# Pairs in the first layer's projections, one mask fewer on GpSimd, and the third layer's first weights listed earlier

## The chip, the cores and the metric

The kernel runs on one core of a Trainium2 chip. The metric is the time of one execution on the device, in microseconds; lower is better. Five engines matter: TensorE (PE, whose weight loads are listed as PEld), VectorE (DVE), ScalarE (ACT), GpSimd (POOL), and SyncE (SP), whose queue issues the DMAs.

## The reference

Three layers in float32, over 4 batches of 576 positions.

- First layer: attention with a feature map. For each of 8 heads, k and q (64 wide) are projected on 128 features, the largest absolute value of each row is subtracted, and exp of both signs is taken. From k come kv (features by values) and z (their sum); the output is q'kv / (q'z + 1e-6).
- Second layer: four attention experts of one head each (causal softmax); each position takes the two experts with the largest gate logits, weighted by a softmax over these two.
- Third layer: eight two-layer experts, 512 to 1024 to 512 with relu. A position's expert is its argmax, or the expert of the position before it where a local gate says so; the output is scaled by that expert's softmax value.

```
e = fresh_e if s == 0 or local_gate[b, s] < 0.5 else prev_e
out[b, s] = p[e] * (np.maximum(x[b, s] @ w1[e], 0.0) @ w2[e])
```

## The kernel before, in words

Instructions are written in program order and put into engine queues by a scheduler that goes by their order in the program as priority, and by when it thinks their inputs are ready. Each engine then works through its queue in order.

**First layer** (class PhaseA). The work is 16 units, one for two heads of one batch, and the steps of three units are interleaved by A_STEPS. `proj` (line 245) projects k ("k", four tiles), the last positions of both ("e", one tile) and q ("q", four tiles): for every tile t there is one matmul per head h, on the upper or the lower 64 rows of the array, into the PSUM tile pt[h]. The tiles of "k" and "q" rotate through five banks (tag X), those of "e" through two (tag mm). `num` (line 370) makes the numerators in two halves of 288 columns, in banks of tag mm, and copies each out to the batch's x1: the first by ACT (line 386), the second by DVE (line 384).

**Second layer** (PhaseB). Five slots run one after the other: s0, s1, x, s2, s3. A main slot works on the two experts that its batch uses most; slot x works on one further expert of one batch (the extra). Each slot is an order of steps written out by hand; that of s2 is

```
    "s2": ("s0b f s0a t t s1a s2a s1b f s2b p0a p0b t t s3a t s3b t p1a f t p1b t p2b p2a f f t p3a f p3b s4a n0 "
            "f v0 s4b p4a n1 t p4b S0a v1 S0b t o0 t S1a S1b o1 o2 o3 t t w"),
```

s is a score, p a transpose of its exponentials, f a projection of the next slot, v the product with the values, o two output products (`wout`, matmuls px in banks of tag mm), S a score of the next slot, and t a tick. `dest` moves px to the batch's x2. The extra's result y has to be added to the batch that it belongs to, which is known only at run time: for each batch b there is a factor hit[b], 1 for that batch and 0 for the others. Batch 0 is added on DVE in slot x itself (line 1274), batch 1 by `adds` on DVE (line 1291); for batches 2 and 3 `adds` writes y times hit to x2 on GpSimd, ahead of the slot (line 1284, sixteen instructions; that of batch 2 over y itself), and `dest` then adds px with a tensor_tensor on DVE (line 1230). `extras` sets hit of batch 3 to 0: it takes no extra.

**Background.** Gates, weight loads and splits run beside the slots. They are generators in lanes of a queue (class Background); a tick lets the first entry of each lane do one step, in the order of the lanes' letters. A `yield n` makes an entry wait n ticks (a plain one: the next tick), an entry with `after` waits until the named entry has left the queue, and `ensure` runs an entry to its end.

**The third layer's start.** `Gates.fresh` (line 593) counts how often each expert is wanted (cnt, line 624, on DVE), waits four ticks, sums the counts over the partitions with one small matmul (hpc, line 627), finds the most wanted expert with five DVE instructions (lines 630 to 635), casts its number (line 698) and has SP load it into a register. The first batch's gate g0 is put in lane r at the start of slot s2. With that register `weights_first` (entry W1_0) loads three pieces of the first weights, 512 KB each (line 1421), and splits each in a high part on ACT (line 1436, w1h) and a rest on DVE (line 1437, w1l). W1_0 is put in lane w at the start of slot s3, and the first f of that slot ensures it. `hidden` (line 1464) then multiplies: for each of 16 pieces 12 matmuls (ph, lines 64 to 66), of which ten pieces stand as f in slot s3. The layer's batches follow, each with 192 matmuls ph and 192 matmuls po on PE.

`Together` (line 69) puts the instructions of a block right behind the first one of them, with raised priority. `issue_after` orders the instructions of a block behind a given one on its engine.

Of the kernel before, what the change touches and what calls it, by code (L numbers as in the profile page):

```python
# [12 lines left out]
AF = mybir.ActivationFunctionType  # L13
OP = mybir.AluOpType
# [5 lines left out]
B, H, S, HD = 4, 8, 576, 64  # L20
# [5 lines left out]
HALF = S // 2  # L26
# [175 lines left out]
class PhaseA:  # L202
# [42 lines left out]
    def proj(self, i, nm):  # L245


        nc, r, after = self.nc, self.st[i], self.bg.tc.issue_after
        w, raws = self.w_phi, r["raw"]
        n = 1 if nm == "e" else 4  # L250
        u = r["u" + nm] = self.p3.tile([128, n, 256], F32, tag=f"u{nm}", name=f"u{nm}_{i}")
        mx = self.p3.tile([128, 2, n], F32, tag=f"mx{nm}", name=f"mx{nm}_{i}")
        if n == 1:
            pt = [self.ps.tile([128, HALF], F32, tag="mm", name=f"pj{nm}_{i}_{h}") for h in range(2)]
        else:
            pt = [self.ps.tile([128, 512], F32, tag="X", name=f"pj{nm}_{i}_{h}") for h in range(2)]
        for t in range(n):
            for h in range(2):
                p = slice(64 * h, 64 * h + 64)
                c = dict(k=0, e=512, q=640)[nm] + 128 * t  # L260
                with ExitStack() as x:
                    if i == 1 and nm != "k":
                        x.enter_context(after(self.kv_last.ins))
                    nc.tensor.matmul(pt[h][:, 128 * t:128 * t + 128], raws[p, c:c + 128], w[p], start=True, stop=True)  # L264
        for step in self.order(i, nm, n):
            if len(step) == 3:
                h, t0, t1 = step
                ins = lambda: nc.vector.tensor_reduce(
                    mx[:, h, t0:t1], pt[h][:, 128 * t0:128 * t1].rearrange("p (t f) -> p t f", f=NF),
                    axis=AX.X, op=OP.max, apply_absolute_value=True)  # L270
            else:
                h = step[0]
                ins = lambda: nc.vector.tensor_tensor(  # L273
                    u[:, :, NF * h:NF * h + NF], pt[h][:, 0:128 * n].rearrange("p (t f) -> p t f", f=NF),
                    mx[:, h, :, None].to_broadcast([128, n, NF]), op=OP.subtract)
            with ExitStack() as x:
                if i == 0 or i == 1 and nm == "k":
                    x.enter_context(after(self.last.ins))
                self.last = ins()
            if len(step) == 1:  # L280
                self.bg.anchor(self.last)
# [88 lines left out]
    def num(self, i, hf):  # L370
        nc, r, (b, p) = self.nc, self.st[i], self.units[i]
        qp, kvs = r["qp"], r["kvs"]
        if p == 0 and hf == 0:
            self.st["x1", b] = self.x1_tile(b)
            self.st["dd", b] = self.dr.tile([H, S], F32, tag="dd", name=f"dd_{b}", bufs=2)
        c = slice(hf * HALF, (hf + 1) * HALF)
        pn = self.ps.tile([128, HALF], F32, tag="mm", name=f"pn_{i}_{hf}")
        with Together(self.bg.tc) as one:
            for sg in range(2):
                for h in range(2):  # L380
                    one(nc.tensor.matmul(pn[64 * h:64 * h + 64, :], kvs[:, sg, 64 * h:64 * h + 64], qp[:, h, sg, c],  # L381
                                         start=sg == 0, stop=sg == 1))
        if hf:
            nc.vector.tensor_copy(self.st["x1", b][:, p, c], pn)
        else:
            nc.scalar.activation(self.st["x1", b][:, p, c], pn, AF.Copy)  # L386

    def den(self, i, hf):
        nc, (b, p) = self.nc, self.units[i]
# [92 lines left out]
class Gates:  # L482
# [110 lines left out]
    def fresh(self, xf, wg32, b, out):  # L593

        nc, ps, k, t = self.nc, self.ps, self.k, self.t
# [26 lines left out]
                                code[:, :, None].to_broadcast([128, QT, NE]), op=OP.is_equal)  # L622
        cnt = t([NE], "cnt8", b)
        nc.vector.tensor_reduce(cnt, hot.rearrange("p t e -> p e t"), axis=AX.X, op=OP.add)
        yield 4
        pc = ps.tile([128, HALF], F32, tag="mm", name=f"hpc_{b}")
        nc.tensor.matmul(pc[:, 0:NE], k.ones, cnt, start=True, stop=True)
        most, e0 = t([1], "most", b), out["e0"]
        c = t([NE], "cnt8", b)
# [424 lines left out]
class PhaseB:  # L1054
# [157 lines left out]
    def main(self, b, q):  # L1212
        nc = self.nc
        s = Slot(self, f"s{b}")
        s.q = q

        def early():
            s.ws = self.g[b]["ws"][:, :, 0:2]
            self.load_w(s, [self.gt.reg(self.g[b]["perm"][0:1, r:r + 1], f"b{b}_{r}", 3) for r in range(2)])
            yield  # L1220
            yield from self.split(lambda ch: self.x1[b][:, ch, :], q, f"b{b}", s.xs)

        def dest(hf, ch, c, px):
            if b not in self.x2:
                self.x2[b] = self.x2["pool"].tile([128, 4, S], F32, tag="x", name=f"x2_{b}")
            if q > self.qx and not (hf or ch):
                self.bg.ensure("adds")
            x2 = self.x2[b][:, ch, c]
            if q > self.qx:
                nc.vector.tensor_tensor(x2, px, x2, op=OP.add)  # L1230
            else:
                nc.scalar.activation(x2, px, AF.Copy)

        s.early, s.dest = early, dest
        return s

    def extra(self, q, nm, regs=None, entry=None):

        nc = self.nc
        s = One(self, nm)  # L1240
# [21 lines left out]
        def tile(b):  # L1262
            self.x2[b] = self.x2["pool"].tile([128, 4, S], F32, tag="x", name=f"x2_{b}")
            return self.x2[b]
# [12 lines left out]
            nc.vector.tensor_tensor(s.x2[:, ch, c], px, s.x2[:, ch, c], op=OP.add)  # L1277

        def adds():

            def scaled(x2, b):
                for ch in range(4):
                    for c in (slice(0, HALF), slice(HALF, S)):
                        nc.gpsimd.tensor_scalar(x2[:, ch, c], s.y[:, ch, c], self.hit[:, b:b + 1], 1.0,
                                                op0=OP.mult, op1=OP.mult)
                    yield

            for b in self.order[1:q]:
                m = self.hit[:, b:b + 1]
                for ch in range(4):  # L1290
                    nc.vector.scalar_tensor_tensor(self.x2[b][:, ch], s.y[:, ch], m, self.x2[b][:, ch],
                                                   op0=OP.mult, op1=OP.add)
                    yield
            for b in self.order[q + 2:]:
                self.bg.ensure(f"early_s{b}")
                yield from scaled(tile(b), b)
            yield from scaled(s.y, self.order[q + 1])

        s.adds = adds if entry is None else None
        s.early, s.dest = early, dest if entry is None else dest_one  # L1300
# [5 lines left out]
    def run(self, slots, order, pc):  # L1306
# [18 lines left out]
        for q, s in enumerate(slots):  # L1325
# [3 lines left out]
            early(q + 2, 9 if q == self.qx else 0)  # L1329
            if q == self.qx + 1:  # L1330
                bg.add("g0", pc.gate(0), False, lane="r")
                bg.add("adds", slots[self.qx].adds(), lane="a")
            if last:
                bg.add("sc", pc.scale(0), lane="r")
                bg.add("h", pc.gate2(0), lane="r")
                bg.add("W1_0", pc.weights_first(), False, lane="w", after=["g0"])
                bg.add("x0", pc.split(self.x2[0], "c0"), False, lane="w")

            def ready():
# [462 lines left out]
```

## Time and profile before

| | us |
|---|---|
| three runs | 545.13, 545.26, 545.91 (median 545.26) |
| the profiled execution | 545.53 |
| its span, first to last instruction | 543.7 |
| PE busy | 518.8 (95% of the span) |
| DVE busy | 362.4 (67%) |
| ACT busy | 263.6 (48%) |
| GpSimd busy | 159.0 (29%) |

The profile is of one execution; its instructions have their lines in the kernel, and idle time of an engine is put down to what ended it. Matmuls are pipelined, so PE's busy time covers stretches in which its instructions overlap. A float32 matmul stands as two records where its weights are float32. The granted clock of TensorE is 1.00 in nearly the whole span; 1.00 is 2.4 GHz and 0.50 is 1.2 GHz. The span divides into the first layer (to about 170 us), the second (to about 335 us, with the third layer's first matmuls from 302 us on) and the third.

### The profile page before, as it was taken

To read this page: it belongs to the slowest core of one execution; us is meant where nothing else is said; L and a number is where in the kernel's file an instruction comes from. 1 tells how busy PE (TensorE), PEld (TensorE's weight loads), DVE (VectorE), ACT (ScalarE), POOL (GpSimd) and SP (SyncE) were. 2 spreads that over 40 slices of the span, in tenths; PEclk is the share of its full clock that TensorE was granted. 3 is DMA by queue.
4 is the path that set the end of the run, shared out by engine and by line. 5 is a ranking of instruction groups with operands and counts; after the bars stand their busy time and mean duration, and the time that the engine had idled before them with its cause. 6 is when DMAs were issued, how large, how long until landed. Compare 5 with 4: busy or idle time off the path is not lost.

```text
span 543.7 us, 11808 instructions
## 1 busy us (share of the span) xinstructions
PE 518.8 (95%) x4456; PEld 437.6 (80%) x4456; DVE 362.4 (67%) x972; ACT 263.6 (48%) x603; POOL 159.0 (29%) x270
## 2 busy tenths in 40 slices
PE   7999999999999998999798899999999999999995
PEld 6766766666676787887586788999999999998995
DVE  7876777977754797987996767742764366527541
ACT  3867566656665467775755553431451235114100
POOL 5665696397477141222546010000000000000000
PEclk9999999999999999999999899999999999999999
DMA  8432373454125026402000601182335133813011
GB/s 245 133 112 88 109 234 101 147 153 156 27 74 182 5 68 184 138 2 79 2 1 10 225 0 47 33 261 99 131 133 177 45 127 133 270 45 127 2 55 39
DMA packets 32709, 57.07 MB, mean 105 GB/s; under 512 B 7012, under 2 KB 17636, under 8 KB 31620
## 3 DMA queue, kind: packets, MB, share of 16 engines
q1 hardware_dynamic: 32644, 56.24, 32.1%
q8 instruction: 37, 0.61, 0.5%
q14 instruction: 28, 0.23, 0.1%
HBM read 41.86 MB, written 14.36 MB: 103 GB/s over the span
## 4 chain that ended last, share of the span: by engine, by line
PE 70%; DVE 12%; ACT 9%; DMA 3%; issue 3%; POOL 2%; SPq 0%; ACTq 0%; DVEq 0%; POOLq 0%
PE po_c L64 6%; PE po_c L65 6%; PE po_c L66 6%; PE ph_c L64 5%; PE pq_s L766 5%; PE ph_c L65 5%; PE ph_c L66 5%; PE Y L332 3%; PE pd L398 3%; PE pn L381 3%; PE pjk L264 2%; PE py_s L913 2%; PE pt_s L885 2%; ACT a_kp L303 2%; DVE uk L273 2%
## 5 line engine op out<-in xcount | busy, mean ns | idle before, releaser
L64 PE MATMUL ph_c<-xh_c,w1h_c 128*128 128x288 f32 x256 | 77.4, 303 | 2.5 <-ACT w1h_c L1436 2.5
L65 PE MATMUL ph_c<-xl_c,w1h_c 128*128 128x288 f32 x256 | 76.2, 298 | 0.0
L64 PE MATMUL po_c<-h_c,w2h_c 128*128 128x288 f32 x256 | 76.1, 297 | 0.0
L66 PE MATMUL ph_c<-xh_c,w1l_c 128*128 128x288 f32 x256 | 75.9, 298 | 0.0
L65 PE MATMUL po_c<-h_c,w2h_c 128*128 128x288 f32 x256 | 75.5, 295 | 0.0
L1484 ACT ACTIVATE h_c<-ph_c 128x288 fp32r<-128x288 f32 x64 | 25.9, 408 | 102.2 <-PE ph_c L66 102.1
L66 PE MATMUL po_c<-h_c,w2l_c 128*128 128x288 f32 x256 | 75.4, 295 | 0.0
L308 POOL TENSOR_TENSOR zs<-a_kp 128x256 f32<-128x256 f32 x64 | 47.6, 757 | 52.9 <-ACT x L386 27.2
L64 PEld LDWEIGHTS ph_c<-xh_c,w1h_c 128*128 128x128 f32 x256 | 48.6, 190 | 4.6 <-ACT w1h_c L1436 2.7
L1485 DVE SCALAR_TENSOR_TENSOR h_c<-ph_c,h_c 128x288 fp32r<-128x288 f32 x64 | 29.0, 456 | 34.0 <-ACT h_c L1484 33.7
L64 PEld LDWEIGHTS po_c<-h_c,w2h_c 128*128 128x128 f32 x256 | 48.1, 188 | 0.9 <-issue 0.9
L65 PEld LDWEIGHTS ph_c<-xl_c,w1h_c 128*128 128x128 f32 x256 | 48.6, 190 | 0.0
L66 PEld LDWEIGHTS ph_c<-xh_c,w1l_c 128*128 128x128 f32 x256 | 48.4, 190 | 0.0
L66 PEld LDWEIGHTS po_c<-h_c,w2l_c 128*128 128x128 f32 x256 | 48.1, 188 | 0.0
L65 PEld LDWEIGHTS po_c<-h_c,w2h_c 128*128 128x128 f32 x256 | 48.1, 188 | 0.0
L766 PE MATMUL pq_s<-xh_b,w_s 128*128 128x288 f32 x192 | 43.6, 305 | 0.8 <-DVE q_s L733 0.4
L1507 DVE TENSOR_TENSOR fo_c<-po_c,pb 128x288 f32<-128x288 f32 x32 | 14.5, 455 | 42.6 <-PE po_c L66 42.6
L332 PE MATMUL Y<-a_kp,a_v 128*64 128x256 f32 x320 | 38.5, 384 | 0.5
L381 PE MATMUL pn<-qp,kvs 128*64 128x288 f32 x256 | 34.6, 408 | 0.3 <-ACT qp L368 0.3
L766 PEld LDWEIGHTS pq_s<-xh_b,w_s 128*128 128x128 f32 x192 | 32.0, 188 | 3.5 <-issue 1.3
L303 ACT ACTIVATE a_kp<-uk 128x1024 f32<-128x1024 f32 x30 | 31.6, 1052 | 6.4 <-DVE uk L273 3.4
L320 ACT ACTIVATE qp<-tr 128x512 f32<-128x512 f32 x64 | 33.6, 634 | 0.6 <-PE tr L318 0.6
(315 smaller groups left out, 1212.9 us busy)
## 6 DMA issues: line engine op xcount, KB each, us to landing
w1raw_c<-in_w_dram SPq DMA_DIRECT2D x16, 512.0 KB, 4.9
w2raw_c<-in_w_dram SPq DMA_DIRECT2D x16, 512.0 KB, 5.1
raw<-in_kq_dram SPq DMA_DIRECT2D x15, 320.0 KB, 3.2
rb<-d SPq DMA_DIRECT2D x32, 144.0 KB, 3.1
x1d<-x SPq DMA_DIRECT2D x4, 1152.0 KB
x2d<-x SPq DMA_DIRECT2D x4, 1152.0 KB
raw<-in_kq_dram SPq DMA_DIRECT2D x16, 256.0 KB, 4.4
a_v<-in_v_dram SPq DMA_DIRECT2D x16, 256.0 KB, 4.1
```

Of the source, the lines that this page charges most:

```text
L64: nc.tensor.matmul(out, lh, rh, start=start, stop=False, **kw)
L65: nc.tensor.matmul(out, lh, rl, start=False, stop=False, **kw)
L66: return nc.tensor.matmul(out, ll, rh, start=False, stop=stop, **kw)
L303: nc.scalar.activation(kp[:, 0:4, sg, :], u[:, 0:4, :], AF.Exp, scale=sc)
L308: add(zs[:, j, sg, :], kp[:, j, sg, :], kp[:, 2 + j, sg, :], op=OP.add)
L320: self.bg.anchor(nc.scalar.activation(qp[:, h, sg, 0:512], tp, AF.Exp, scale=sc))
L332: self.kv_last = one(nc.tensor.matmul(Y[64 * h:64 * h + 64, 0:256], vt[:, t, h, :], kp[:, t, :, h * NF:(h + 1) * NF], start=t == 0, stop=t ...
L381: one(nc.tensor.matmul(pn[64 * h:64 * h + 64, :], kvs[:, sg, 64 * h:64 * h + 64], qp[:, h, sg, c], start=sg == 0, stop=sg == 1))
L398: nc.tensor.matmul(pd[32 * h:32 * h + 32, :], r["kvs"][:, 2, o:o + 32], r["qp"][:, h % 2, sg, c], start=sg == 0, stop=sg == 1)
L766: self.nc.tensor.matmul(out, self.wqkv[t][:, wj, ch, 0:m], x[:, ch, c], start=wj == ch == 0 and x is xh, stop=wj == 1 and ch == 3)
L1484: nc.scalar.activation(hh[:, c], ph, AF.Relu),
L1485: nc.vector.scalar_tensor_tensor(hl[:, c], ph, 0.0, rd(hh[:, c]), op0=OP.max, op1=OP.subtract))
```

## The change

In `proj` the two heads of a tile become a pair, head 1 first, and each pair is ordered behind the one before. In `num` the two engines change places. In `fresh` the wait ahead of the sum is two ticks for batch 0 and four for the others. In `dest` of a main slot, slot s2 (q == qx + 1) computes x2 = x2 * hit + px in one DVE instruction, where x2 is y itself; slot s3 only copies px, the first half on ACT and the second on DVE; `adds` keeps batch 1 alone, and the sixteen GpSimd instructions of line 1284 are gone. W1_0 is put in lane w at the start of slot s2, behind g0.

```diff
         for t in range(n):
-            for h in range(2):
-                p = slice(64 * h, 64 * h + 64)
-                c = dict(k=0, e=512, q=640)[nm] + 128 * t
-                with ExitStack() as x:
-                    if i == 1 and nm != "k":
-                        x.enter_context(after(self.kv_last.ins))
-                    nc.tensor.matmul(pt[h][:, 128 * t:128 * t + 128], raws[p, c:c + 128], w[p], start=True, stop=True)
+            c = dict(k=0, e=512, q=640)[nm] + 128 * t
+            with ExitStack() as x:
+                if i == 1 and nm != "k":
+                    x.enter_context(after(self.kv_last.ins))
+                if t:
+                    x.enter_context(after(mm.ins))
+                one = x.enter_context(Together(self.bg.tc))
+                for h in (1, 0):
+                    p = slice(64 * h, 64 * h + 64)
+                    mm = one(nc.tensor.matmul(pt[h][:, 128 * t:128 * t + 128], raws[p, c:c + 128], w[p], start=True, stop=True))
...
         if hf:
+            nc.scalar.activation(self.st["x1", b][:, p, c], pn, AF.Copy)
+        else:
             nc.vector.tensor_copy(self.st["x1", b][:, p, c], pn)
-        else:
-            nc.scalar.activation(self.st["x1", b][:, p, c], pn, AF.Copy)
...
-        yield 4
+        yield 4 if b else 2
         pc = ps.tile([128, HALF], F32, tag="mm", name=f"hpc_{b}")
...
-            if q > self.qx and not (hf or ch):
-                self.bg.ensure("adds")
             x2 = self.x2[b][:, ch, c]
-            if q > self.qx:
-                nc.vector.tensor_tensor(x2, px, x2, op=OP.add)
+            if q == self.qx + 1:
+                if not (hf or ch):
+                    self.bg.ensure("adds")
+                nc.vector.scalar_tensor_tensor(x2, x2, self.hit[:, b:b + 1], px, op0=OP.mult, op1=OP.add)
+            elif q > self.qx and hf:
+                nc.vector.tensor_copy(x2, px)
             else:
                 nc.scalar.activation(x2, px, AF.Copy)
...
         def adds():
-
-            def scaled(x2, b):
-                for ch in range(4):
-                    for c in (slice(0, HALF), slice(HALF, S)):
-                        nc.gpsimd.tensor_scalar(x2[:, ch, c], s.y[:, ch, c], self.hit[:, b:b + 1], 1.0,
-                                                op0=OP.mult, op1=OP.mult)
-                    yield
-
             for b in self.order[1:q]:
...
-            for b in self.order[q + 2:]:
-                self.bg.ensure(f"early_s{b}")
-                yield from scaled(tile(b), b)
-            yield from scaled(s.y, self.order[q + 1])
...
             if q == self.qx + 1:
                 bg.add("g0", pc.gate(0), False, lane="r")
+                bg.add("W1_0", pc.weights_first(), False, lane="w", after=["g0"])
                 bg.add("adds", slots[self.qx].adds(), lane="a")
             if last:
                 bg.add("sc", pc.scale(0), lane="r")
                 bg.add("h", pc.gate2(0), lane="r")
-                bg.add("W1_0", pc.weights_first(), False, lane="w", after=["g0"])
```

## Rows read from the trace of the kernel before

**Rows 1.** The page: busy time by engine, and PE in 40 slices

```profile
PE 518.8 (95%) x4456; PEld 437.6 (80%) x4456; DVE 362.4 (67%) x972; ACT 263.6 (48%) x603; POOL 159.0 (29%) x270
...
PE   7999999999999998999798899999999999999995
```

**Rows 2.** Busy us by stretch: length, PE, PEld, DVE, ACT, POOL, PEclk, DMA, GB/s

```profile
100.00:120.00 20.00, 19.21 (x210) 13.17 (x210) 17.04 (x38) 14.67 (x31) 12.25 (x15) 1.00 0.61 190
...
260.00:280.00 20.00, 17.04 (x120) 13.60 (x121) 19.29 (x44) 12.73 (x40) 11.49 (x22) 1.00 0.01 1
280.00:300.00 20.00, 17.34 (x131) 13.96 (x128) 14.47 (x49) 10.23 (x33) 9.80 (x18) 1.00 0.07 20
300.00:320.00 20.00, 17.69 (x120) 16.38 (x121) 14.66 (x36) 11.26 (x25) 1.12 (x4) 0.91 0.40 140
```

**Rows 3.** Waits of PE: total us, times, longest us

```profile
PE ph_c L64 <- ACT w1h_c L1436: 2.5, 1, 2.5
...
PE pc L561 <- DVE cnt L558: 1.3, 2, 1.0
PE px_s L64 <- DVE x L1230: 1.1, 2, 0.8
...
PE pg L500 <- DVE x L1274: 0.8, 1, 0.8
...
PE pje L264 <- DVE x L384: 0.6, 1, 0.6
```

**Rows 4.** The chain of waits, 292 to 303 us: start, us, what

```profile
292.85 0.32 PE hpc L627 x2
...
297.62 3.56 DMA w1raw_c<-in_w_dram
301.20 1.06 ACT w1h_c L1436
302.31 0.41 PE ph_c L64
```

**Rows 5.** DVE in order of time: start, us

```profile
281.73 0.21 DVE L624 TENSOR_REDUCE cnt<-hot 128x8 f32<-128x40 f32 x1
...
296.42 0.13 DVE L698 CAST ri_c<-c_e 1x1 int32<-1x1 f32 x1
...
302.29 1.23 DVE L1437 TENSOR_TENSOR w1l_c<-w1raw_c,w1h_c 128x1024 fp32r<-128x1024 f32 x1 [1.19 <-ACT w1h_c L1436]
```

**Rows 6.** ACT in order of time, at the end of slot s2

```profile
299.74 0.63 ACT L1189 ACTIVATE woh_s<-wor_s 128x512 fp32r<-128x512 f32 x1 [5.12 <-PE px_s L65]
```

**Rows 7.** Busy us by stretch around the fall of the clock

```profile
302.80:306.10 3.30, 3.30 (x15) 2.99 (x14) 2.15 (x3) 1.96 (x4) 0.00 (x0) 0.50 0.60 195
306.20:308.00 1.80, 1.80 (x16) 1.80 (x16) 1.41 (x3) 1.66 (x4) 0.00 (x0) 1.00 0.25 68
```

**Rows 8.** The adding of the extra to batch 0 on DVE: ns min/median/max

```profile
L1274 DVE SCALAR_TENSOR_TENSOR x<-x,x_m,x x4: 805/1054/1056, 265.8 to 268.7; 128x576 f32<-128x576 f32 x4
```

**Rows 9.** GpSimd's masks: ns min/median/max

```profile
L1284 POOL TENSOR_SCALAR x<-x,x_m x16: 504/505/1003, 261.7 to 279.6; 128x288 f32<-128x288 f32 x16
```

**Rows 10.** PE in order of time: a unit of the first layer's steady part

```profile
43.91 1.16 PE L264 MATMUL pjk<-a_w,raw 64*128 64x128 f32 x16
44.91 0.39 PE L264 MATMUL pje<-a_w,raw 64*128 64x128 f32 x4
```

**Rows 11.** PE in order of time: a unit beside the second layer's gates

```profile
107.37 0.37 PE L264 MATMUL pjq<-a_w,raw 64*128 64x128 f32 x1
...
108.83 0.37 PE L264 MATMUL pje<-a_w,raw 64*128 64x128 f32 x1 [0.63 <-DVE x L384]
...
109.91 0.44 PE L358 MATMUL kvt<-ident,ue 128*128 128x128 f32 x2
```

**Rows 12.** DVE by line, 18 to 160 us: numerators' copies

```profile
L384 DVE COPY x<-pn 128x288 f32<-128x288 f32 x14 | 6.3, 453 | 13.3 <-PE pn L381 13.3
```

**Rows 13.** ACT by line, 18 to 160 us: numerators' copies

```profile
L386 ACT ACTIVATE x<-pn 128x288 f32<-128x288 f32 x14 | 5.5, 395 | 0.8 <-PE pn L381 0.8
```

## The prediction

> **What bounds the kernel now.** I read the page first: PE is busy in 95% of the span, and among the forty slices those below nine tenths lie at the start, at the end, at 204 us, and in a dip between 258 and 313 us [rows 1]. The table by stretch says how deep it is: PE is idle 2.96 us in 260 to 280, 2.66 us in 280 to 300 and 2.31 us in 300 to 320, beside 0.79 us in 100 to 120 [rows 2]. Outside the dip a change that gives PE no less work can gain next to nothing; inside it there are 7.9 us. The waits of PE name what ended that idle time: one wait of 2.5 us for the first high part of the third layer's weights, and smaller ones for DVE [rows 3]. Then the chain of waits, in order of time: the small sum hpc at 292.85, DVE's search behind it, the weights' DMA from 297.62 for 3.56 us, ACT's split for 1.06 us, and the first ph at 302.31 [rows 4]. So that wait is the end of a chain that begins with hpc, and hpc stands late by order alone: its input cnt was ready at 281.73 + 0.21 = 281.94 us, 10.9 us earlier [rows 5].
>
> **The sum, and the load that hangs on it.** In slot s2 the gate's first seven steps take the first seven ticks; four ticks more put hpc at the eleventh, behind the last transposes, and two ticks put it at the ninth, behind the projections. The entry g0 leaves its lane a tick after the sum, and since lane r comes before lane w, W1_0 issues its first two loads at the tenth tick, the third load and the first split at the twelfth. On SP nothing else stands between, and the three buffers that the loads fill are those of slot s3's weights, read for the last time by projections that stand before the ninth tick. I estimate hpc at 283 to 285 us: not before cnt, 281.94, and about where those projections end. From hpc to the first ph the chain took 302.31 - 292.85 = 9.46 us [rows 4]; at that length the first weights are split by 292.5 to 294.5 us, five us or more before PE is through with px, whose matmuls end about 2.47 us before the first ph. The wait goes whole: **-2.5 us**. The bounds are 0 and that wait.
>
> The splits move too: three of 1.06 us on ACT [rows 4] and three of 1.23 us on DVE [rows 5]. They used to lie where PE had stopped; now they lie in 290 to 300 us, among the ends of slot s2. ACT has room, it was idle 5.12 us just there [rows 6], and DVE was busy 14.47 of 20 us in 280 to 300 [rows 2]. They can still stand in front of an eviction of px, and a split whose load has not landed holds back what is queued behind it. Against that, the search behind hpc leaves that place, and PE waited 1.1 us for the evictions there [rows 3]. I put the two against each other at **0**, between -1.1 and +1.23 (one DVE split in the way).
>
> Moved early, hpc may find cnt not ready, and PE's queue stands behind it. The second layer's gates have the same sum at two ticks: four of them, of which two waited, 1.3 us together and 1.0 us at the most [rows 3]. I take the mean, 1.3 / 4: **+0.3 us**, between 0 and 1.0.
>
> **The clock.** The granted clock was 0.50, the level of 1.2 GHz, in 302.80 to 306.10, right after PE had stood still for 2.47 us, and 1.00 again after it [rows 7]. In the slow stretch 15 matmuls began in 3.30 us, 0.220 each; after it 16 in 1.80 us, 0.1125 each. At full clock the fifteen take 1.7 us: **-1.6 us** if PE no longer stops, 0 if it stops elsewhere as long.
>
> **GpSimd's masks.** Sixteen instructions of 0.505 us (median) go [rows 9]. Their own time is beside the path; what counts is DVE next to them, since DVE is busy 19.29 of 20 us in 260 to 280 and PE waits for it there [rows 2, 3]. The adding of the extra to batch 0 took 1.055 us three times and 0.805 us the fourth time, when GpSimd had paused [rows 8]: 3 x 0.25 = 0.75 us, directly ahead of the gate's first matmuls, which waited 0.8 us for it [rows 3]. I take **-0.75 us**, between 0 and -1.5. The lower end is three whole masks, 3 x 0.505. The Trainium skill, SBUF — State Buffer, section Who interferes with whom, says that a DVE instruction with two SBUF inputs and a GpSimd instruction that reads SBUF cannot run together, and that the second waits until the first has finished. By that rule the term would be that lower end, and the sum 0.75 us lower; the trace shows half of it, and I go by the trace.
>
> DVE's new x2 * hit + px in slot s2 replaces an instruction of the same shape, and slot s3's eight sums become four copies on each engine: 0, hidden beside ph, as PE's idle time in that slot is gone from 320 us on (slices of 9 in rows 1).
>
> **The pairs.** In the steady part of the first layer the heads run as pairs already: sixteen records of pjk begin in 44.91 - 43.91 = 1.00 us [rows 10]. Only beside the gates the pairs break up. In the worst unit, e and q, twenty records, take from 107.37 to 109.91 = 2.54 us [rows 11], where 20 x 1.00 / 16 = 1.25 us would do: 1.3 us, of which 0.63 us is one wait for the numerators' copy on DVE. Four other places lose a pair's time or so, 2 x 1.00 / 16 = 0.125 us each. That bounds the gain at 1.8 us. But DVE is busy 17.04 of 20 us in that stretch [rows 2], so the chain there runs through DVE, and PE's saving is mostly waited away: I take a fifth, **-0.4 us**. The other end is a loss: a pair waits for the later of two banks, at the 0.63 us of that row once more, +0.6.
>
> **The numerators' copies.** The copies last 0.453 us on DVE and 0.395 on ACT [rows 12, 13]; each engine still does one of a unit's two, and PE works on beside them: 0. The second one, for whose bank e waited, now leaves by ACT; that is in the bound above.
>
> **The sum.** -2.5 + 0 + 0.3 - 1.6 - 0.75 - 0.4 = -4.95 us. The profiled execution took 545.53, of which 543.7 are its span; it stands 0.27 us above the median of 545.26. The forecast for the median is 545.26 - 4.95 = 540.3 us.
>
> **The rivals.**
>
> *The gap fills further.* With weights at hand from 293 us on, PE can put ph between the px that wait for evictions, and DVE's gain carries through. Then the terms go to their lower ends: 2.5 + 1.1 + 1.6 + 1.5 + 1.2 = 7.9 less, 537.4 us. For it: PE was idle 2.66 us in 280 to 300 [rows 2]. Against it: ph and px share two banks, and px has priority. 14%.
>
> *The gain is passed on.* PE no longer waits for weights, but for slot s2's last evictions behind DVE's splits; the wait is halved and the clock still falls, or DVE stays the bound in 260 to 300. I reckon half of the 4.95 us: 542.8 us. For it: DVE's 19.29 of 20 us. 20%.
>
> *The load is not earlier.* If SP reads the register or ACT takes the split no sooner (a split placed behind slot s2's exponentials in ACT's queue, the loads behind a buffer), the change doesn't do what it says, and only the terms of masks and pairs remain, -1.15: 544.1 us. Against it: nothing in SP's queue or in the buffers stands in the way. 10%.
>
> *Slower: the pairs stall.* Each pair is now issued as one, and PE's queue stands until both banks are free. If every unit then waits as the one of rows 11 did, 0.63 us in 15 units is 9.5 us, less the 4.95: 549.8 us. It decides from 4.95 / 15 = 0.33 us a unit. Against it: in the steady part no such wait stands among PE's [rows 3], and the banks change hands long before. For it: at the start DVE is the later one. 6%. The Trainium skill, TensorEngine Tiling (Array Packing), section Gotcha 1: PSUM Pressure, says that row tiles working side by side need banks of their own and that this raises the pressure on PSUM; that is this rival's mechanism, and the trace shows it in one unit of sixteen.
>
> **How the numbers follow.** The forecast's own case has 50%, from 539 to 541.8 us. The range, 537.4 to 544.2 us, takes in the first two rivals and the third one's centre; what lies outside is the slower rival and the tails, less than 2 in 10. A measurement of this kernel can tell some 0.2% (1.1 us) from no change. Faster by more: forecast and the first two rivals, 0.84. Within: the third, 0.10. Slower: 0.06.
>
> **What would show it.** Right: hpc near 284 us and the first w1raw issue near 288 us; no wait of ph for w1h over 0.5 us; a granted clock of 1.00 from 300 to 310 us; the adding of the extra at 0.8 us four times; pjq of one length in all units. Wrong: PE's idle time in 260 to 320 us still over 6 us, a stretch at 0.50 after the start, or waits of pj for copies in many units.

## The result, and the profile after the change

The changed kernel takes 540.25 us (median of 4 runs, 539.98 to 541.20) where the kernel before took 545.59 beside it (545.13 to 546.37): ratio 0.9904, 95% interval 0.9886 to 0.9921. The forecast was 540.3 us, range 537.4 to 544.2. The profiled execution took 539.98 us, of which 538.2 are its span.

The page of the changed kernel, its busy times, PE's slices and the granted clock, beside [rows 1]:

```profile
PE 516.0 (96%) x4456; PEld 436.2 (81%) x4456; DVE 359.3 (67%) x968; ACT 264.5 (49%) x607; POOL 150.2 (28%) x254
...
PE   7999999999999999999999899999999999999995
...
PEclk9999999999999999999999999999999999999998
```

The dip between 258 and 313 us has become one slice of 8. The stretches, with the columns of [rows 2]:

```profile
260.00:280.00 20.00, 17.78 (x125) 14.21 (x126) 19.12 (x51) 13.74 (x44) 1.98 (x7) 1.00 0.00 1
280.00:300.00 20.00, 18.30 (x141) 14.92 (x139) 16.54 (x42) 12.37 (x32) 10.00 (x17) 1.00 0.45 140
300.00:320.00 20.00, 19.56 (x153) 18.07 (x153) 14.65 (x46) 10.44 (x29) 1.41 (x5) 1.00 0.05 21
```

PE is idle 2.22 + 1.70 + 0.44 = 4.36 us here, where it was 7.93 before [rows 2]: 3.57 less. No stretch is at 0.50 any more (0.91 in 300 to 320 before). POOL's 11.49 us have become 1.98, since the masks are gone. The waits of PE over the whole run (total us, times, longest us):

```profile
PE pc L564 <- DVE cnt L561: 1.4, 2, 1.1
...
PE pje L267 <- DVE x L389: 1.1, 1, 1.1
...
PE px_s L64 <- DVE x L1233: 0.7, 1, 0.7
PE pd L401 <- DVE x L389: 0.7, 1, 0.7
...
PE pg L503 <- DVE q_s L736: 0.5, 1, 0.5
```

The wait of 2.5 us for the first weights [rows 3] is in no row, nor is a wait of hpc. Three instructions in order of time (start, us): DVE's count, PE's sum hpc, and the load in SP's queue:

```profile
279.88 0.22 DVE L627 TENSOR_REDUCE cnt<-hot 128x8 f32<-128x40 f32 x1
...
282.19 0.29 PE L630 MATMUL hpc<-cnt,ones 128*128 128x8 f32 x2
...
285.63 7.62 SPq L1414 DMA_DIRECT2D w1raw_c<-in_w_dram  x4
```

hpc runs at 282.19 us (292.85 before, [rows 4]), two microseconds behind its count, and the first piece's load goes out at 285.63. What has taken the wait's place is seen on DVE, in order of time (start, us):

```profile
291.25 1.63 DVE L1430 TENSOR_TENSOR w1l_c<-w1raw_c,w1h_c 128x1024 fp32r<-128x1024 f32 x1 [0.78 <-ACT w1h_c L1429]
...
293.18 0.50 DVE L1233 SCALAR_TENSOR_TENSOR x<-x,x_m,px_s 128x288 f32<-128x288 f32 x1
293.60 1.63 DVE L1430 TENSOR_TENSOR w1l_c<-w1raw_c,w1h_c 128x1024 fp32r<-128x1024 f32 x1
295.15 1.05 DVE L925 TENSOR_TENSOR yl_s<-by_s,yh_s 128x288 fp32r<-128x288 f32 x1
296.13 0.93 DVE L1233 SCALAR_TENSOR_TENSOR x<-x,x_m,px_s 128x288 f32<-128x288 f32 x2
296.98 1.21 DVE L1430 TENSOR_TENSOR w1l_c<-w1raw_c,w1h_c 128x1024 fp32r<-128x1024 f32 x1
298.12 0.93 DVE L1233 SCALAR_TENSOR_TENSOR x<-x,x_m,px_s 128x288 f32<-128x288 f32 x2
```

The splits of the second and third piece (w1l, 1.63 and 1.21 us) now stand between the evictions that px waits for. Slot s2's px begin at 292.11 us (293.95 before) and end at 300.64 (299.84 before).

**A ruler for small differences.** Up to the extra row's last px the run hangs on DMAs whose landing varies (shown below with the pairs). That px ends at 265.49 us in one profile of the changed kernel and at 265.88 in another, and between 265.47 and 266.58 in the nine that share the changed first layer. So I measure each profile also by its *middle stretch*: from the end of the last px of the extra row to the end of batch 0's last ph. It was 81.94 us before and is 76.76 after; a second profile of the changed kernel gave 76.74. In six kernels (load alone, masks back, before filled and the three with the splits behind) two of batch 0's po come ahead of the end mark and lengthen the stretch by about 0.1 us: from the mark to batch 1's last ph these take 55.31 to 55.38 us, the others 55.42 to 55.45. All runs:

| kernel | median us | ratio to before, 95% interval | middle stretch us |
|---|---|---|---|
| before | 545.59 | | 81.94 |
| changed | 540.25 | 0.9904, 0.9886 to 0.9921 | 76.76 |
| changed, again | 540.55 | 0.9892, 0.9875 to 0.9910 | 76.74 |
| listed late | 541.15 | 0.9908, 0.9893 to 0.9923 | 76.76 |
| sum late | 545.25 | 0.9986, 0.9973 to 0.9999 | 82.35 |
| load alone | 541.30 | 0.9907, 0.9893 to 0.9921 | 77.55 |
| masks back | 541.08 | 0.9909, 0.9894 to 0.9924 | 77.51 |
| no pairs | 541.62 | 0.9913, 0.9894 to 0.9931 | 76.74 |
| no swap | 541.19 | 0.9908, 0.9891 to 0.9924 | 76.78 |
| before, filled | 544.93 | 0.9976, 0.9963 to 0.9989 | 80.58 |
| sum sooner | 542.95 | 0.9948, 0.9931 to 0.9966 | 79.73 |
| splits behind | 539.65 | 0.9881, 0.9860 to 0.9902 | 75.36 |
| splits behind, adds 4 later | 539.48 | 0.9873, 0.9857 to 0.9890 | 75.99 |
| splits behind, adds 8 later | 539.26 | 0.9866, 0.9850 to 0.9883 | 75.37 |

The first two rows come from one comparison. The kernel before took 546.04 to 546.21 us in the others, so kernels of different comparisons stand beside each other by ratio and stretch.

### The profile page after: what moved, and what is told of

It reads as the page before. It is cut to its first block, busy times and chain, and to the rows that moved or that the text cites. A ratio compares the mean times of both kernels' runs of the same rounds, so it can differ in the third digit from the quotient of the medians.

```text
span 538.2 us, 11790 instructions
## 1 busy us (share of the span) xinstructions
PE 516.0 (96%) x4456; PEld 436.2 (81%) x4456; DVE 359.3 (67%) x968; ACT 264.5 (49%) x607; POOL 150.2 (28%) x254
## 4 chain that ended last, share of the span: by engine, by line
PE 79%; DVE 11%; ACT 5%; DMA 2%; issue 2%; POOL 0%; SPq 0%; ACTq 0%; DVEq 0%; POOLq 0%
PE po_c L64 6%; PE po_c L65 6%; PE po_c L66 6%; PE Y L335 6%; PE ph_c L64 5%; PE pq_s L769 5%; PE pn L384 5%; PE ph_c L66 5%; PE ph_c L65 5%; PE pjk L267 3%; PE pd L401 3%; PE py_s L916 2%; PE tr L321 2%; PE pt_s L888 2%; PE pjq L267 2%; PE pg L503 2%
```

## The experiments

**The listing alone, undone.**

```diff
                 bg.add("g0", pc.gate(0), False, lane="r")
-                bg.add("W1_0", pc.weights_first(), False, lane="w", after=["g0"])
...
                 bg.add("h", pc.gate2(0), lane="r")
+                bg.add("W1_0", pc.weights_first(), False, lane="w", after=["g0"])
```

> The changed kernel with the first weights' load listed at slot s3's start again, as before; the sum of batch 0 stays two steps sooner. My theory (the load hangs on the sum alone, and nothing stands in front of it on SP): hpc stays near 282.2 us, the first w1raw issue near 285.6 us, the first ph near 292.6 us, and the time stays within 0.6 us of the changed kernel's 540.25. Rival (the listing decides when the load goes out): the first w1raw issue falls behind 295 us, the wait of ph for w1h comes back at about 2.5 us, and the time is near 544.3 us.

hpc at 282.17, the first load at 285.60, the first ph at 292.60 us, middle stretch 76.76. The median is 0.9 us above the first one of the changed kernel, more than the 0.6 I had allowed, but beside a slower kernel before (546.21); the ratio, 0.9908 to 0.9904, is the same within its interval. The listing does nothing: nothing stands on SP in front of the load either way, so the sum alone decides.

**The sum alone, undone.**

```diff
-        yield 4 if b else 2
+        yield 4
```

> The changed kernel with the sum of batch 0 four steps behind its count again; the early listing stays. My theory (the sum decides): hpc is back near 292 us, the first w1raw issue near 296 us, ph waits for w1h by 2 to 2.5 us and stands at a granted clock of 0.50 for some 3.3 us behind it, and the time is 3.5 to 4.5 us above the changed kernel's 540.25, 543.8 to 544.8 us. Rival (PE's idle time between 260 and 320 us only moves; DVE and not the load bounds that stretch): not more than 2 us above.

hpc 292.33, load from 297.27 us. The wait and the slow clock are back. PE's wait in this kernel:

```profile
PE ph_c L64 <- ACT w1h_c L1429: 2.5, 1, 2.5
```

Two stretches behind it, with the columns of [rows 2]:

```profile
303.00:307.00 4.00, 4.00 (x18) 3.68 (x18) 2.04 (x4) 1.94 (x5) 0.00 (x0) 0.50 0.44 144
307.00:307.60 0.60, 0.60 (x5) 0.60 (x4) 0.60 (x1) 0.40 (x1) 0.00 (x0) 0.50 1.10 137
```

By ratio this costs (0.9986 - 0.9904) x 545.59 = 4.5 us, by the stretch 5.59, more than I had expected: PE stayed at 0.50 from 301.8 to past 307.6 us, over 5.8 us, where before it was 3.3 [rows 7], after a wait of the same length. The rival (not over 2 us) is out.

**The load alone, on the kernel before**: the sooner sum and the early listing, nothing else of the change.

```diff
-        yield 4
+        yield 4 if b else 2
...
+                bg.add("W1_0", pc.weights_first(), False, lane="w", after=["g0"])
...
-                bg.add("W1_0", pc.weights_first(), False, lane="w", after=["g0"])
```

> The kernel before with the sooner sum and the early listing alone: no pairs for k, no swapped copies, GpSimd's masks kept. My theory (wait 2.5 and clock 1.6 go, as the prediction's first terms say): 4.1 us below the kernel before, 541.3 to 541.5 us; hpc near 283 us, the first ph near 293.5 us, no stretch at 0.50 behind 300 us. Rival (without the masks gone, DVE is too late to use the load: the gain is passed on to slot s2's evictions): 2 us below at the most, 543.3.

The stretch is 77.55, which is 4.39 us below before; the ratio is 0.9907. By the stretch this part is 4.39 of the 5.18 us; by the ratio it cannot be told from the whole change (0.9904). The adding of the extra still takes 3.74 us for its four instructions, and the load is used all the same: the gain is not passed on.

**GpSimd's masks back**, with the adding in two steps and slot s3's sums on DVE.

```diff
...
-                nc.vector.scalar_tensor_tensor(x2, x2, self.hit[:, b:b + 1], px, op0=OP.mult, op1=OP.add)
-            elif q > self.qx and hf:
-                nc.vector.tensor_copy(x2, px)
+            if q > self.qx:
+                nc.vector.tensor_tensor(x2, px, x2, op=OP.add)
...
+            for b in self.order[q + 2:]:
+                self.bg.ensure(f"early_s{b}")
+                yield from scaled(tile(b), b)
+            yield from scaled(s.y, self.order[q + 1])
```

> The changed kernel with GpSimd's sixteen masks, the two-step adding and slot s3's eight sums on DVE back as before. My theory as put in the prediction (DVE's adding of the extra to batch 0 is slowed by GpSimd and stands ahead of the gate): the four L1274-like instructions take 1.05 us three times again, and the time is 0.75 us above the changed kernel, 541.0. By the trace of the changed kernel, in which slot s2's px begin 1.84 us sooner than before, it could be as much as 1.7 us. Rival (what DVE loses there is given back, since PE has ph to fill the gaps behind it): within 0.3 us of the changed kernel.

The adding to batch 0 on DVE, in order of time, in this kernel:

```profile
265.79 3.75 DVE L1277 SCALAR_TENSOR_TENSOR x<-x,x_m,x 128x576 f32<-128x576 f32 x4
```

The same in the changed kernel:

```profile
265.39 3.00 DVE L1279 SCALAR_TENSOR_TENSOR x<-x,x_m,x 128x576 f32<-128x576 f32 x4
```

The four cost 0.75 us more, the figure taken from [rows 8]. Slot s2's px begin 1.05 us later (counted from the extra's last px), and 0.75 us of it is left at the end of the stretch, 0.65 at batch 1's last ph. The rival (within 0.3 us) is out by the stretch; by ratio alone (0.9909) it could not be told.

**The kernel before with PE kept busy through the wait.**

The lines that keep slot s2's last product as px_mm are left out here.

```diff
...
     def front(self, n):
 
+        if n == 0:
+            fill = self.ps.tile([128, 512], F32, tag="tr", name="fill")
+            xh = self.xs[0]
+            with self.bg.tc.issue_after(self.pb.px_mm.ins), self.bg.tc.high_priority():
+                for _ in range(17):
+                    self.nc.tensor.matmul(fill[:, 0:HALF], xh[:, 0, 0:128], xh[:, 0, 0:HALF], start=True, stop=True)
```

> The kernel before with seventeen matmuls more behind slot s2's last px, on a bank that nobody reads, so that PE works through the wait for the first weights; nothing else is changed, and the output does not use them. My theory (PE fell to 0.50 because it stood still for 2.47 us): the first ph begins at 302.3 us as before, the granted clock stays at 1.00 behind it, and batch 0's last ph ends 1.6 us sooner than the kernel before's 347.56; the time is 1.6 us below the kernel before's in the same comparison. Rival (the clock falls there for another reason): the stretch at 0.50 stays, and the time is that of before within 0.4 us.

PE in order of time in this kernel:

```profile
298.81 0.29 PE L66 MATMUL px_s<-yh_s,wol_s 128*128 128x288 f32 x1
298.94 2.40 PE L1466 MATMUL fill<-xh_c 128*128 128x288 f32 x17
301.27 0.40 PE L64 MATMUL ph_c<-xh_c,w1h_c 128*128 128x288 f32 x1
301.51 0.30 PE L65 MATMUL ph_c<-xl_c,w1h_c 128*128 128x288 f32 x1
...
304.41 0.38 PE L66 MATMUL ph_c<-xh_c,w1l_c 128*128 128x288 f32 x1
```

The last of these lines in the kernel before:

```profile
307.03 0.38 PE L66 MATMUL ph_c<-xh_c,w1l_c 128*128 128x288 f32 x1
```

Two stretches of the filled kernel, with the columns of [rows 2]:

```profile
302.00:304.00 2.00, 2.00 (x16) 1.78 (x15) 1.90 (x3) 1.51 (x3) 0.20 (x1) 1.00 0.36 68
304.00:306.00 2.00, 2.00 (x18) 2.00 (x17) 1.67 (x4) 1.89 (x4) 0.00 (x0) 1.00 0.77 262
```

The clock stays at 1.00 although nothing useful was added: it was the standing still that took it down. The stretch falls by 1.36 us, the median by 1.1, the ratio says 1.3. But the first ph came 1.04 us sooner than before, which I had not expected (DVE's queue came out in another order and finished the search sooner), so the stretch holds that and the clock in one sum. The price on the spot can be read from the lines above: from the first ph to the ph at 304.41 it took 3.14 us here, and 4.72 us to the same ph before (302.31, [rows 4], to 307.03), with nearly the same work between (two transposes here, three scores there): 1.58 us. From the first ph to batch 0's last, though, only 0.24 us is left, 45.01 us beside 45.25: eight more matmul records (six transposes of slot s3 and two po) fall between them here, and PE idles 0.32 us. So the run shows the cause of the slow clock and what it costs where it falls, and not that all of this reaches the end.

**The pairs alone, undone.**

```diff
...
-                one = x.enter_context(Together(self.bg.tc))
-                for h in (1, 0):
-                    p = slice(64 * h, 64 * h + 64)
-                    mm = one(nc.tensor.matmul(pt[h][:, 128 * t:128 * t + 128], raws[p, c:c + 128], w[p], start=True, stop=True))
+            for h in range(2):
...
+                    nc.tensor.matmul(pt[h][:, 128 * t:128 * t + 128], raws[p, c:c + 128], w[p], start=True, stop=True)
```

> The changed kernel with the first layer's projections issued head by head again, as before; all else stays. By the term of the prediction: 0.4 us above the changed kernel, with the units beside the gates broken up again. My theory now, from the milestones of the changed kernel (the first layer ended 0.88 us sooner than before, but at the extra row's scores only 0.12 us of that was left): the last pn ends 0.3 to 0.9 us later than 177.81 us, and from 228 us on both stand within 0.2 us of each other, so the time is the same within 0.3 us. Rival (the pairs cost what their stalls cost): faster than the changed kernel by 0.5 us or more.

**The swap alone, undone.**

```diff
         if hf:
-            nc.scalar.activation(self.st["x1", b][:, p, c], pn, AF.Copy)
-        else:
             nc.vector.tensor_copy(self.st["x1", b][:, p, c], pn)
+        else:
+            nc.scalar.activation(self.st["x1", b][:, p, c], pn, AF.Copy)
```

> The changed kernel with the numerators' copies on their old engines (the second half on DVE, the first on ACT). The prediction's term was 0: the same time as the changed kernel within 0.5 us, and from the extra row's last px to batch 0's last ph the same 76.76 us within 0.1. Rival (it was the swap that shortened the first layer, not the pairs): the last pn ends 0.4 us later or more, with waits of PE for L389's copies in the units beside the gates.

Both are the same in the stretch (76.74 and 76.78), and in the first layer they tell the parts apart. From the third unit's first pjk to the last unit's the kernel before takes 133.89 us; pairs alone 133.81, swap alone 133.34, both 133.03. Each of three units that hold the denominators takes 10.44 us with the swap and 10.76 without, pairs or not. One such place, PE in order of time, in the kernel before:

```profile
32.80 0.43 PE L341 MATMUL Y<-zs,ones 128*32 128x128 f32 x8
33.34 2.15 PE L398 MATMUL pd<-qp,kvs 128*32 128x288 f32 x32
```

The same in the changed kernel:

```profile
32.97 0.43 PE L344 MATMUL Y<-zs,ones 128*32 128x128 f32 x8
33.21 2.12 PE L401 MATMUL pd<-qp,kvs 128*32 128x288 f32 x32
```

pd begins 0.54 us behind Y's start before and 0.24 after. The copy that frees pd's bank, and what stands ahead of it on ACT, in the kernel before:

```profile
31.95 1.04 ACT L303 ACTIVATE a_kp<-uk 128x1024 f32<-128x1024 f32 x1
32.90 0.39 ACT L386 ACTIVATE x<-pn 128x288 f32<-128x288 f32 x1
```

And on DVE in the changed kernel:

```profile
32.12 0.46 DVE L389 COPY x<-pn 128x288 f32<-128x288 f32 x1 [0.43 <-PE pn L384]
```

On ACT the first half's copy stood behind an exponential of 1.04 us; on DVE it goes at once. Three times 0.32 would be 0.96 us, but with the swap PE also waits 0.7 us in another unit, pd for a numerators' copy (the row of pd in the waits above), which is in no kernel without it. So the swap was worth something, and the pairs next to nothing. None of it reaches the middle stretch: the extra's last px ends at 265.47 to 266.58 us in the nine profiles with the changed first layer, and at 265.61, 265.70 and 265.93 in the three with the old one. The chain of waits where the extra row begins, in the changed kernel (start, us, what):

```profile
211.51 4.15 DMA rb<-d
...
215.75 0.58 DVE x L434
...
218.36 1.75 PE pq_x L769 x11
```

The same chain in the kernel without pairs:

```profile
211.55 5.32 DMA rb<-d
...
216.97 0.58 DVE x L431
...
219.57 0.53 PE pq_x L766 x2
```

PE comes to the extra's projections by way of a DMA, and that DMA began at the same time in both kernels and took 4.15 us in one and 5.32 in the other. My expectation that both would stand within 0.2 us from 228 us on fell on this: they stood 1.2 apart. The last pn ended at 178.18 us without the pairs, inside what I had expected, but it lay between 177.55 and 178.86 in the nine profiles that share the changed first layer, so that tells nothing; nor does the ratio, 0.9913, tell a kernel without pairs from one with them. Without the swap the last pn ended at 179.28, behind all of those nine: the rival, that the swap shortened the first layer, was right, and the stretch is the same as I had expected.

**The splits behind the evictions** (the second and third piece only). The lines that keep slot s2's last eviction as px_out are left out here.

```diff
...
+            with ExitStack() as x:
+                if lay == 1 and nm == "c0" and 0 < g < 3:
+                    x.enter_context(self.bg.tc.issue_after(self.pb.px_out.ins))
-            nc.vector.tensor_tensor(lo, raws[g], rd(h), op=OP.subtract)
+                nc.vector.tensor_tensor(lo, raws[g], rd(h), op=OP.subtract)
```

> The changed kernel with DVE's splits of the second and third piece of the first weights (1.63 and 1.21 us there) placed behind the last of slot s2's eight evictions. My theory (in the changed kernel DVE is the bound from 292 to 300 us, and those two splits stand between the evictions that px waits for; the first ph's need the first piece alone): slot s2's last px ends 1.5 to 2.5 us sooner than 300.64, PE's idle time in 292 to 300 us, 1.2 us, goes, and the time is 0.7 to 1.2 us below the changed kernel, 539.0 to 539.6. Rival (PE only moves its ph from the gaps to behind px, and waits for the second piece instead): within 0.3 us, with a wait of ph for w1l.

DVE in order of time in this kernel:

```profile
298.54 0.93 DVE L1233 SCALAR_TENSOR_TENSOR x<-x,x_m,px_s 128x288 f32<-128x288 f32 x2
299.39 2.35 DVE L1433 TENSOR_TENSOR w1l_c<-w1raw_c,w1h_c 128x1024 fp32r<-128x1024 f32 x2
```

A stretch of it, with the columns of [rows 2]:

```profile
296.00:300.00 4.00, 3.95 (x30) 3.56 (x28) 3.57 (x8) 1.57 (x4) 0.00 (x0) 1.00 0.12 47
```

The same stretch of the changed kernel:

```profile
296.00:300.00 4.00, 2.84 (x20) 2.40 (x20) 4.00 (x9) 0.45 (x2) 0.00 (x0) 1.00 0.62 166
```

PE was idle 1.16 us there with DVE at 4.00 of 4 us; now 0.05 us, and slot s2's last px ends at 298.85 (300.64 before this edit). No wait for w1l appears. The stretch is 75.36, 1.40 us shorter than the changed kernel's; the ratio 0.9881 says 1.3. The intervals of the two ratios overlap, the stretch settles it.

**The sum one step sooner still.**

```diff
-        yield 4 if b else 2
+        yield 4 if b else 1
```

> The changed kernel with the sum of batch 0 one step behind its count, not two. My theory (the first ph is bounded by px and by DVE's split now, not by the load): hpc and the load come about 1 us sooner, DVE's three splits fall among slot s2's transposes and reductions, and the time is that of the changed kernel within 0.5 us. Rival (the load still decides): 0.5 to 1 us below. Other rival (hpc is now ahead of its input and holds PE's queue): a wait of hpc for cnt, and slower by it, 0.3 to 1 us.

None of the three: 2.97 us slower by the stretch, 2.4 by ratio, and not by a wait of hpc. The wait of PE that is new:

```profile
PE pt_s L888 <- ACT pT_s L901: 1.2, 1, 1.2
```

Two stretches of this kernel, with the columns of [rows 2]:

```profile
276.00:280.00 4.00, 2.57 (x17) 1.80 (x16) 3.92 (x17) 2.86 (x8) 1.67 (x5) 1.00 0.00 0
280.60:283.60 3.00, 3.00 (x15) 2.81 (x15) 1.38 (x8) 0.00 (x0) 0.00 (x0) 0.50 0.00 0
```

hpc came at 282.55 us, 0.5 us sooner if counted from the extra's last px. With it listed a step earlier, twenty-four projection matmuls of slot s3 went behind it in PE's queue (36 stand ahead of it, 60 in the changed kernel): the second half of k, and twelve of the values behind it. The twelve of k had filled the time in which the transposes wait for ACT, so PE stood 1.43 us of the 4.00, and the clock fell behind it. The load was never what this step was about: the order on PE was.

**The adding to batch 1 put off by four and by eight ticks**, on top of the splits behind:

```diff
-                bg.add("adds", slots[self.qx].adds(), lane="a")
+                bg.add("adds", slots[self.qx].adds(), lane="a", wait=4)
```

> The version with the two splits behind the evictions, and in it the adding of the extra to batch 1 begins four ticks later, so that its four instructions of 0.73 to 0.81 us no longer stand ahead of the gate's logits on DVE. My theory (in 266 to 278 us DVE is full, and pg, pq and the scores wait for it): PE's idle time between 260 and 280 us, 2.3 us, falls by 0.3 to 0.8, and the time by as much below the version without it, 538.9 to 539.4 us by the scale on which that one stood at 539.65. Rival (DVE's work there is all due before the next px anyway, and moving it only moves the wait): within 0.2 us.

> The same with eight ticks: the adding to batch 1 falls behind the gate's count, into 280 to 292 us, where DVE has gaps of 0.6 and 0.5 us. My theory: hpc's input is ready some 2 us sooner, the idle time between 260 and 280 us falls by 0.5 to 1.2 us, and the time by as much. Rival (DVE then stands in front of the transposes' copies and the maxima of slots s2 and s3, and slot s2's px begin later): nothing is gained against the version with the two splits behind, or up to 1 us is lost.

PE's idle time in 260 to 280 us falls from 2.30 to 1.86 and 1.93, and in 280 to 300 it rises from 0.80 to 1.70 and 1.71. The stretch is 0.63 us longer than without with four ticks (75.99) and the same with eight (75.37). The wait moved. With four ticks the idle time fell as I had forecast, but the stretch grew, which neither my theory nor its rival had. With eight ticks the stretch shows no gain, as the rival said. The ratios (0.9873, 0.9866) lie lower than 0.9881, but well inside each other's intervals, and from the extra's last px to the end of the span the three take 271.41, 271.86 and 271.00 us; whether eight ticks gain 0.4 us behind the stretch stays open. I would keep the plainest, the one with the splits behind alone.

**The changed kernel again.**

> The changed kernel itself, so that the three others stand beside it on the same chip: the same ratio to the kernel before as in its first timing, 0.990 within its interval. A spread of a microsecond in the last pn's end and in the extra's first projection, as the kernels with the same first layer have shown, with the same 76.76 us from the extra row's last px to batch 0's last ph within 0.1.

It came out so: 0.9892 in its interval, stretch 76.74. The last pn's end (177.55) and the extra's first projection (218.76) lie 0.26 and 0.40 us from those of the first profile, less than the microsecond I had named.

## Why the prediction was right

**The middle stretch closes the account.** It is 81.94 - 76.76 = 5.18 us shorter. The whole of it, with the columns of [rows 2], in the kernel before:

```profile
265.61:347.56 81.95, 75.04 (x557) 64.29 (x556) 63.55 (x170) 40.62 (x104) 19.41 (x39) 0.98 0.16 53
```

And in the changed kernel:

```profile
265.49:342.25 76.76, 73.31 (x556) 62.78 (x556) 60.60 (x165) 41.53 (x108) 13.33 (x28) 1.00 0.17 56
```

PE is idle 6.91 us in the one and 3.45 in the other, 3.46 less (the 3.57 further up counts some that lies ahead of the mark); what remains, 1.73 us, is busy time, which I put down to work that no longer runs at 0.50. The unfilled kernels without a slow stretch are busy 72.76 to 73.48 us there, so this is good to some 0.4 us. By the terms:

- *The wait, -2.5.* Right: no row of it is left. hpc came at 282.19 us, a little before the 283 to 285 I had estimated, and the load at 285.63, where I had named 288.
- *The clock, -1.6.* Right: 1.73 by the account above, 1.58 beside the filled kernel, which also shows the cause. It is a price of this one run, though: with the same wait the slow stretch lasted over 5.8 us in the kernel with the late sum.
- *hpc waiting for its count, +0.3.* Wrong: 0. cnt was done at 280.10 us (281.94 before, [rows 5]), two microseconds ahead of hpc.
- *The masks, -0.75.* Right: 0.75 in the adding, 0.75 in the stretch (0.65 at batch 1's last ph). From the rule of the Trainium skill, SBUF — State Buffer, section Who interferes with whom, I had worked out twice as much, three whole masks. That price was mine: when the adding's second and third instructions begin, the mask in progress has 0.45 us left by its recorded end, and they take 0.25 us longer (see the last section).
- *The splits against the search, 0.* Right as a sum. The idle time not accounted for is 3.46 - 2.5 - 0.75 = 0.2 us of gain. But the splits do cost something: the version with two of them moved is 1.40 us shorter. What paid for it was only argued: ph filling gaps between px, and the search leaving that place.
- *The pairs, -0.4, and the copies, 0.* Wrong step. The pairs alone saved 0.08 us of the first layer and the swap 0.55, together 0.86, and none of it arrives: the extra's projections wait for a DMA. I had bounded the pairs by the one mixed unit, and its wait did not shrink but grew (0.63 to 1.1 us, DVE's copy there still stands behind xl_b and w_s); the unit's q takes 2.83 us there and 1.06 in most units, so the sign of one length for all did not come. I had looked for the swap's worth in the copies' lengths and not in what they stand behind on ACT.

So the total, -4.95 forecast and -5.34 measured between the medians, is good because the large terms of the middle stretch are. That it is as close as this is luck: the 0.4 of the pairs, which did not arrive, about makes up for the 0.3 that hpc did not cost and the 0.2 that came besides.

**The rivals.** *The gap fills further* came in part: twelve ph run between px from 292.61 to 295.4 us, then none until 300.48. What I had held against it, the shared banks, fits the code; no run tried another sharing, so it is not shown that this stopped them. In its sum I had put the pairs at 1.2 us, though my own bound for them was 1.8. *The gain is passed on* named the right place, slot s2's evictions behind DVE's splits, but not its size: the clock did not fall there. *The load is not earlier* is out. *The pairs stall* is out: one wait of pje at 1.1 us and no others like it. The kernel without the swap has that wait too (1.1), the one without the pairs 0.6, so the pairs lengthened it. That is the rival's mechanism in one unit of sixteen.

## What to carry to other kernels

Where PE waits for the end of a chain, look for the first link that stands late by order alone; moving one small sum gave 4.4 of 5.2 us, and the earlier listing beside it nothing. When the waited-for work moves earlier, look at what it is put in front of: here two splits that could wait cost 1.4 us between evictions, and one step too early pushed PE's filler behind the sum and lost 3 us. Measure small parts between two points of the trace that lie behind the last variable DMA, since the whole run varies by more than they are worth.

## What the runs showed of the hardware that I had not expected

**DVE and GpSimd take turns.** Two groups of the changed kernel over the whole run (ns min/median/max, first and last start): GpSimd's split xl_c, and DVE's yl_s.

```profile
L1447 POOL TENSOR_TENSOR xl_c<-x,xh_c x8: 793/804/1787, 286.5 to 294.1; 128x288 fp32r<-128x288 f32 x8
...
L925 DVE TENSOR_TENSOR yl_s<-by_s,yh_s x8: 428/459/1055, 206.4 to 325.1; 128x288 fp32r<-128x288 f32 x8
```

The longest xl_c starts at 294.11 us, while DVE's w1l is under way (293.60 to 295.23, shown above), and takes 1.787 us where 0.804 is usual: longer by 0.98 us, when w1l still had 1.12 us to run. That w1l itself took 1.63 us instead of 1.21, beside the xl_c before it, which had 0.55 us left, and yl_s behind it 1.055 instead of 0.459, when the long xl_c had 0.74 us left. Each is longer by what the other had left, less 0.13 to 0.15 us (0.2 us in the adding to batch 0). Up to this difference it agrees with the rule of the Trainium skill, SBUF — State Buffer, section Who interferes with whom, that the later of the two waits until the earlier is done. So a long instruction on either engine is paid for by its neighbour with nearly what is left of it.

**The slow clock's length varies.** After PE had stood 2.47 us (before), 2.5 (late sum) and 1.43 of 4.00 us (sum sooner), the stretch at 0.50 lasted 3.3 us, over 5.8 and at least 3.0. Two waits of 0.70 and 0.47 us in 296 to 299 us of the changed kernel brought no fall. The Trainium skill, TensorE: Matmul & The Clock Gate, Part 1, says that the number of matmuls at the slow clock at a kernel's start differs between runs of one kernel; the traces here show a differing length in the middle of two kernels with the same wait. The times fit: over twelve runs each, the kernel with the late sum spreads by 3.46 us, and the filled one, which has no slow stretch there, by 2.02.

**One DMA, two lengths.** rb<-d, a transfer of 144 KB, took 4.15 us in one profile of the changed kernel and 5.13 in the other. In the kernel without pairs it took 5.32, begun 0.04 us from the first and behind the same issues on SP. No run here shows why.
